# Block-sparse attention and FFN in one kernel: the lead-in's steps in another order, eleven of them ahead of the first unit

## The chip, the cores and the metric

The kernel runs on one core of a Trainium2 chip. The metric is the device time of the whole program in microseconds. Five engines work at the same time, each through its own queue: TensorE (PE; its weight loads are listed as PEld), VectorE (DVE), ScalarE (ACT), GpSimd (POOL) and SyncE (SP), which here issues nearly all DMAs.

## What is computed

Attention over 4 batches, 8 heads, 768 positions and 64 dimensions, with a mask of blocks of 32: a block of queries sees its own block and its neighbours, the first and the last block, and three blocks given as data in `sampled_blocks`. Queries of the first and the last block see all. Then an FFN of 3072 tokens, 512 to 2048 to 512, with h - tanh(h) between.

```python
mask = np.abs(blk_i - blk_j) <= window
mask = mask | (blk_i == 0) | (blk_j == 0) | (blk_i == n_blocks - 1) | (blk_j == n_blocks - 1)
for qb in range(n_blocks):
    for kb in sampled_blocks[qb]:
        mask[qb * block:(qb + 1) * block, kb * block:(kb + 1) * block] = True
...
attn = np.exp(scores)
attn = attn / (np.sum(attn, axis=-1, keepdims=True) + 1e-09)
...
h = x @ w_in
g = h - np.tanh(h)
return (g @ w_out).astype(np.float32)
```

## The kernel before

The tokens are cut into six chunks of 512 (`CHUNKS`: four blocks of 32 for each of 4 batches). The FFN goes through 96 **units**, a unit being one chunk and one tile of 128 of the 2048 inner columns: `first` makes h in bank 4 or 5 of PSUM with 12 products of 128x512, `bent` the function on ScalarE, VectorE and GpSimd in eleven operations (w, t, hs, th, p1, qq, mk, p2, p3, cp, gh, gl), `second` adds another 12 products to banks 0 to 3, two and a half units later. The first eight units are of chunk 0, units 8 to 23 of chunk 1, and so on.

The attention goes through 112 **steps** (class `Unit`): a step is one block of queries and one half-set c (two of the four batches with all heads; K, Q and V are laid out by half-set), and for the edge blocks a third of all keys. A step reads K from `kr`, a buffer of 256 keys that is gathered out of the resident K (`ks`), and V from `vw`, which is gathered by DMA out of HBM. There are two such buffers (`u.i` 0 and 1). A buffer holds three slots for near blocks, the first and the last block, and three sampled blocks; `fresh` copies only what has changed since the buffer's last step, so a step that stays in its half-set fetches one or two near blocks and three sampled ones, and one that changes the half-set fetches everything (seven DMAs of V, seven copies of K or fewer). The sampled ones need indices: `load_samples` fetches the samples and VectorE turns them into offsets (`kx`, `vx`) in some fifteen small operations.

A step then does: `scores` (32 products on PE into two banks), `most` (two maxima on DVE), `exps` (per half one small scaling and two exponentials on ACT), `turn` (eight transposes on PE), `copy` (two copies on ACT), `accum` (64 products on PE with V), `norm` (four operations on DVE) and `put` (a copy on ACT and a subtraction on POOL that hand the result to the FFN as x). The weights come as 64-bit words and are converted in the kernel: `load` fetches a tile, `convert` has three parts on DVE, `split` one operation on ACT and one on POOL.

Every operation is entered into a plan by `at(time, f, ...)`, with a time in units of the FFN, and the plan is sorted and written out. `InOrder` keeps each engine in the order of the plan (the SP queue among them), so the order by hand is the order on the chip; only the waits between engines are found by the framework. Steps below `LEAD` lie ahead of unit 0, by the formula `t(x) = (n + x - T0) * RATE`; those after it have a first time and a spacing by chunk in `BAND`. With `LEAD` 10 and `T0` 10.25, steps 0 to 7 end ahead of unit 0, and 8 and 9 have their `accum` at 0.52 and 1.15. Then six steps of chunk 1 follow at 0.75, 1.89 and so on, 1.14 apart, up to unit 8. Conversions of the first weights stand at four places ahead of unit 0 and at twelve in units 0 to 7 (`CONVA`), with a bank of PSUM for what lies between their parts (`CONVAB`).

The order of the lead-in before: steps 0 to 3 are blocks 1 to 4 of half-set 0, steps 4 to 7 the same blocks of half-set 1, 8 and 9 block 5 of each; the buffers alternate. The SP queue issues K of half-set 0 in four DMAs, Q of step 0, the samples, Q of steps 1 to 3, V of step 0, K of half-set 1 in four DMAs, V of step 1, and then what the plan asks for: Q (four buffers), V of step n+2 after `accum` of step n, and weights. The gathers of K stand on VectorE for steps 0 and 1 and on GpSimd for all others (the sampled blocks always on GpSimd).

Of the kernel before, what the change touches and what calls it, by code (L numbers as in the profile page):

```python
# [23 lines left out]
B, H, S, D = 4, 8, 768, 64  # L24
# [6 lines left out]
CT = 4  # L31

NU = NTOK // P // CT * NFT

LEAD, T0, RATE = 10, 10.25, 0.62
QUICK, TURN, PROD = (0.66, 0.95), 1.0, 1.33
NQ = 4
KEPT = 3
# [8 lines left out]
SEGS = [(0, 0, HALF), (1, 0, HALF), (1, HALF, NFT), (0, HALF, NFT)] + [(n, 0, NFT) for n in range(2, len(CHUNKS))]  # L47
UNITS = [(n, ft) for n, a, b in SEGS for ft in range(a, b)]
ENDS = [sum(b - a for _, a, b in SEGS[: i + 1]) for i in range(len(SEGS))]
BAND = [None, (0.75, 1.14), (22.72, 1.14), (31.87, 1.44), (47.71, 1.44), (63.55, 1.44)]  # L50
EDGES = {3: (0,), 4: (1,), 5: (2, 3)}
LATE = 71.0
CONVA = [0.1, 0.75, 1.4, 2.05, 2.65, 3.31, 3.77, 4.45, 4.91, 6.05, 7.19, 7.62]
CONVAB = [3, 3, 3, 3, 6, 7, 6, 7, 6, 6, 6, 6]
CONVB = 8.35, 0.94

THR2 = 0.16
# [59 lines left out]
class Unit:  # L117
# [3 lines left out]
    def __init__(self, n, c, time, b=None, f=None, k=None, quick=False):  # L121
        self.n, self.c, self.b, self.f, self.k = n, c, b, f, k
        early = n < LEAD
        if early:
            t = lambda x: (n + x - T0) * RATE
            self.t = dict(s=t(0.3), m=t(0.65), e1=t(1.1), e0=t(1.2), turn=t(2.0), c0=t(2.15), c1=t(2.2), pv=t(2.6), norm=t(3.05))
            if n == LEAD - 2:
                self.t.update(pv=0.52, norm=0.6)
            elif n == LEAD - 1:
                self.t.update(turn=0.38, c0=0.43, c1=0.44, pv=1.15, norm=1.25)  # L130
        else:
            t = lambda x: time + x
            turn, prod = QUICK if quick else (TURN, PROD)
            self.t = dict(s=t(0), m=t(0.08), e1=t(0.2), e0=t(0.3), turn=t(turn), c0=t(turn + 0.06), c1=t(turn + 0.05), pv=t(prod), norm=t(prod + 0.1))
        if n < LEAD - 2:
            self.banks = dict(s=((6, 7), (0, 1))[n % 2], t=(2, 3), o=4 + n % 2)
        elif n == LEAD - 1:
            self.banks = dict(s=(0, 1), t=(0, 1), o=2)
        else:
            self.banks = dict(s=(6, 7), t=(2, 3) if early else (6, 7), o=7)  # L140

    def at(self, half, j):

        return (half, self.b) if self.b else (self.f, (NB - 1) * half)


class Attention:
    def __init__(self, tc, k, q, v, samp, rows, ffn, ident, banks, att, sm, f2, rv, at):
# [14 lines left out]

        def add(c, time, **kw):
            u = Unit(len(units), c, time, **kw)
            u.i, u.before = c, last.get(c)
            if u.n < LEAD - 2:
                u.i, u.before = u.n % 2, units[u.n - 2] if u.n > 1 else None
            elif u.n < LEAD:
                u.before = units[u.n - 2]  # L170
            if u.b:
                last[c] = u
            units.append(u)

        for c in range(2):
            for b in CHUNKS[0]:
                add(c, 0, b=b)
        for m, blocks in list(enumerate(CHUNKS))[1:]:
            steps = [(c, dict(b=b, quick=m < 3)) for b in blocks if 0 < b < NB - 1 for c in range(2)]
            edges = [(g // 2, dict(f=g % 2, k=k)) for g in EDGES.get(m, ()) for k in range(3)]  # L180
            steps += edges
            for i, (c, kw) in enumerate(steps):
                add(c, BAND[m][0] + BAND[m][1] * (i - 2 * (m == 1)), **kw)
        lead = lambda x: (x - T0) * RATE
        at(lead(-8.97), self.load_q, units[0])
        for bt in range(B):
            at(lead(-9), self.load_k, 0, bt)
        at(lead(-8.95), self.load_samples, samp, rows)
        for c, t in ((1, lead(-2.5)),):
            for bt in range(B):  # L190
                at(t, self.load_k, c, bt)
        for u in units:
            t, n = u.t, u.n
            if u.b:
                if n:
                    at(max(t["s"] - 2.0, units[n - NQ].t["s"] + 0.01) if n >= NQ else lead(-8.95 + 0.01 * n), self.load_q, u)
                at(max(t["s"] - 1.2, u.before.t["s"] + 0.01 if u.before else lead(-3)), self.gather_k, u)
                at(max(t["s"] - 2.0, u.before.t["pv"] + 0.01 if u.before else lead(-3)), self.gather_v, u)
            else:
                if u.k == 0:  # L200
                    at(units[n - 1].t["s"] + 0.02, self.load_q, u)
                at(units[n - 2].t["pv"] + 0.02, self.load_ve, u)
            at(t["s"], self.scores, u)
            at(t["m"], self.most, u)
            at(t["e1"], self.exps, u, 1)
            at(t["e0"], self.exps, u, 0)
            at(t["turn"], self.turn, u)
            at(t["c1"], self.copy, u, 1)
            at(t["c0"], self.copy, u, 0)
            at(t["pv"], self.accum, u)  # L210
            at(t["norm"], self.norm, u)
            if u.b:
                for x in "hl":
                    at(t["norm"] + (0.1 if x == "h" else 0.15), self.put, u, x)
            elif u.k == 2:
                at(t["e0"] + 0.12, self.weigh, u)
                end = 2 * u.c + u.f in EDGES[len(CHUNKS) - 1]
                quiet = iter([t["norm"] + 0.1 + 0.08 * j for j in range(6)] if end else self.quiet(units[u.n + 1 :], t["norm"]))
                for k in range(3):
                    for s in range(1 + k):  # L220
                        at(next(quiet), self.join, u, k, s)
                for i in range(2):
                    for x in "hl":
                        at(t["norm"] + 0.65 + 0.2 * i if end else LATE + 0.5 * (2 * u.c + u.f) + 0.25 * i, self.put, u, x, i)
# [5 lines left out]
            yield max((u + 0.56 + 0.04 * i for i in range(6)), key=lambda x: min([1] + [abs(x - y) for y in near]))  # L230

    def kr(self, u):
        key = u.i, u.n < 8 + CT * 2
        if key not in self.krs:
            self.krs[key] = self.att.tile([P, H, 256], F32, tag=f"kr{u.i}", name=f"kr{u.i}_{u.n}")
            self.held.pop(("k", u.i), None)
        return self.krs[key]

    def vw(self, u):
        key = u.i, u.n < 8 + CT * 2  # L240
        if key not in self.vws:
            self.vws[key] = [self.att.tile([P, B, VW], F32, tag=f"vw{u.i}{x}", name=f"vw{u.i}{x}_{u.n}") for x in range(2)]
            self.held.pop(("v", u.i), None)
# [8 lines left out]
        return self.loans[i // 2][:, i % 2]  # L252

    def load_k(self, c, bt):
        self.nc.sync.dma_start(out=self.ks[:, c, 2 * bt : 2 * bt + 2], in_=self.k[c][:, 2 * bt : 2 * bt + 2])

    def load_q(self, u):
        for b in (u.b,) if u.b else (0, NB - 1):
# [57 lines left out]
    def gather_k(self, u):  # L316
        nc, i = self.nc, u.i
        k, to = self.ks[:, u.c], self.kr(u)
        e = nc.vector if u.n < 2 else nc.gpsimd
        for s, b, n in self.fresh(("k", i), u, self.near(u) + [(3, 0), (4, NB - 1)]):  # L320
            o = slice(32 * s, 32 * (s + n)) if s < 4 else slice(131, 256, 4)
            e.tensor_copy(out=to[:, :, o], in_=k[:, :, 32 * b : 32 * (b + n)])
# [152 lines left out]
class FFN:  # L475
# [154 lines left out]
    def plan(self, at):  # L630
# [1 line left out]
        banks = [x.bitcast(I32) for x in self.banks]  # L632
        halves = [sorted(((m, ft) for ft in range(a, a + HALF) for m in "io"), key=lambda w: w[1] + NEED[w[0]]) for a in (0, HALF)]
        halves[1].insert(13, halves[1].pop(12))
        slots = [(t(3.3 + 1.6 * k), 0.3 * RATE, None) for k in range(4)] + [(x, 0.09, banks[b]) for x, b in zip(CONVA, CONVAB)]
        slots += [(CONVB[0] + CONVB[1] * k, 0.12, banks[6 + k % 2]) for k in range(2 * HALF)]
        free = []
        for k, ((m, ft), (t0, dt, tmp)) in enumerate(zip(halves[0] + halves[1], slots)):
# [75 lines left out]
```

## Time and profile before

| | us |
|---|---|
| median of three runs | 794.02 (793.66 to 796.94) |
| the profiled execution | 797.82 |
| its span, first to last instruction | 796.1 |
| PE busy in the span | 742.5 (93%) |
| DVE, ACT, POOL busy | 544.1, 478.0, 335.0 |

A span is read in stretches: a table of stages gives the busy time of each engine between two times from the span's start, the chain of waits follows what released what, and the timeline gives instructions in order with the idle time ahead of each and who ended it. Nearly all instructions are issued by one helper, so all have line 78 and are told apart by their tiles: `ps` is a bank of PSUM, `kr<-ks` a gather of K, `vw<-v` one of V, `ps<-kr,q` scores, `m<-ps` most, `ps<-ident,p` turn, `pt<-ps` copy, `ps<-vw,pt` accum, `rs`, `x`, `xt` norm, `ps<-x,wri` the first product of a unit with resident weights, `cvti` and `cvto` the last part of a conversion.

### The profile page before, as it was taken

The page shows a single profiled execution, that of the slowest core. Times are in us where ns is not written, and L with a number is a line of the kernel's source. Part 1 is how long each engine was busy: PE and PEld are TensorE (multiplying, and loading weights), DVE is VectorE, ACT ScalarE, POOL GpSimd, SP SyncE. Part 2 cuts the span into 40 slices and gives each one's busy share as a digit, 9 for nine tenths or more (in the row PEclk, how much of TensorE's full clock was granted, in tenths as well). Part 3 has the DMA queues.
Part 4 walks back from the last instruction along what each step waited for, and adds up shares of the span by engine and source line. Part 5 has one row for each costly group of instructions (what it writes and reads, how often), then busy time and mean ns, then how long its engine had stood idle before and what let it go on. Part 6 is the DMA issues. An engine that isn't in the chain of part 4 may idle for free.

```text
span 796.1 us, 20648 instructions
## 1 busy us (share of the span) xinstructions
PE 742.5 (93%) x8128; PEld 564.5 (71%) x8128; DVE 544.1 (68%) x970; ACT 478.0 (60%) x1021; POOL 335.0 (42%) x406
## 2 busy tenths in 40 slices
PE   0668888999999999999999999999999999999996
PEld 0445656777877777777777777777777777888885
DVE  2565886777986666776666778666676666866654
ACT  0566776667767677566565566565664656554543
POOL 2684666567796555343312334422242211222211
PEclk9878999999999999999999999999999999999998
DMA  7987675399694765475737156666147355236542
GB/s 255 334 226 232 222 226 170 142 331 328 242 276 159 215 216 195 135 230 163 267 115 227 51 173 212 204 224 208 46 129 264 134 200 187 106 106 239 185 159 79
DMA packets 54835, 155.48 MB, mean 195 GB/s; under 512 B 9171, under 2 KB 15828, under 8 KB 54740
## 3 DMA queue, kind: packets, MB, share of 16 engines
q1 hardware_dynamic: 54356, 153.65, 58.7%
q8 instruction: 64, 1.05, 0.5%
q10 hardware_dynamic: 384, 0.52, 0.2%
q14 instruction: 31, 0.25, 0.1%
HBM read 133.17 MB, written 20.97 MB: 194 GB/s over the span
## 4 chain that ended last, share of the span: by engine, by line
PE 75%; DVE 9%; ACT 5%; DMA 4%; POOL 3%; issue 2%; SPq 1%; POOLq 0%; DVEq 0%
PE ps L78 75%; DVE ps L78 4%; DMA vw<-v 2%; ACT pt L78 1%; SPq L78 1%; ACT p L78 1%; DMA ks<-k 1%; DMA room<-rows 1%; DVE m L78 1%; POOL gl L78 1%; DVE cvto L78 1%; POOL kr L78 1%; DVE cvti L78 1%; POOL t L78 1%; DVE t L78 1%
## 5 line engine op out<-in xcount | busy, mean ns | idle before, releaser
L78 PE MATMUL ps<-x,wi 128*128 128x512 f32 x888 | 228.3, 398 | 0.0
L78 POOL TENSOR_TENSOR gl<-t,gh 128x512 fp32r<-128x512 f32 x96 | 124.2, 1294 | 240.4 <-ACT gh L78 123.9
L78 PEld LDWEIGHTS ps<-x,wi 128*128 128x128 f32 x888 | 162.5, 188 | 42.4 <-issue 7.4
L78 PE MATMUL ps<-wo,gh 128*128 128x512 f32 x592 | 190.9, 404 | 0.0
L78 PEld LDWEIGHTS ps<-wo,gh 128*128 128x128 f32 x592 | 107.0, 188 | 30.9 <-issue 7.4
L78 PE MATMUL ps<-wo,gl 128*128 128x512 f32 x296 | 117.0, 397 | 2.8 <-POOL gl L78 2.8
L78 ACT ACTIVATE u<-ps 128x512 f32<-128x512 f32 x96 | 57.2, 596 | 90.1 <-PE ps L78 89.3
L78 POOL COPY kr<-ks 128x256 f32 (+2 forms) x188 | 96.8, 611 | 19.8 <-DVE kr L78 14.5
L78 DVE TENSOR_REDUCE m<-ps 128x2 f32<-128x512 f32 x112 | 72.1, 685 | 40.8 <-PE ps L78 38.4
L78 PE MATMUL ps<-kr,q 64*32 64x256 f32 x1408 | 59.9, 410 | 23.8 <-POOL kr L78 17.9
L78 POOL TENSOR_TENSOR x<-xt,x 128x256 fp32r<-128x256 f32 (+1 forms) x48 | 34.5, 720 | 111.7 <-ACT x L78 108.8
L78 DVE TENSOR_TENSOR ps<-ps,u 128x512 f32<-128x512 f32 x96 | 66.5, 693 | 16.5 <-ACT t L78 16.5
L78 DVE COPY_PREDICATED t<-mk,ps 128x512 f32<-128x512 int32 x96 | 71.4, 743 | 7.4 <-POOL t L78 0.6
L78 ACT ACTIVATE p<-ps,nb 128x256 f32<-128x256 f32 x176 | 73.9, 471 | 3.0
L78 DVE TENSOR_TENSOR t<-t,ps 128x512 f32<-128x512 f32 x64 | 43.7, 683 | 46.6 <-ACT t L78 46.5
L78 DVE SCALAR_TENSOR_TENSOR ps<-qq,ps 128x512 f32<-128x512 f32 x96 | 66.4, 691 | 8.4 <-ACT qq L78 2.7
L78 ACT ACTIVATE qq<-u,bias 128x512 f32<-128x512 f32 x96 | 69.6, 725 | 0.0
L78 ACT ACTIVATE mk<-u,bias 128x512 f32<-128x512 f32 x96 | 69.4, 723 | 0.0
L78 PEld LDWEIGHTS ps<-wo,gl 128*128 128x128 f32 x296 | 55.6, 188 | 18.4 <-POOL gl L78 5.3
L78 DVE SCALAR_TENSOR_TENSOR ps<-u,ps 128x512 f32<-128x512 f32 x96 | 66.3, 691 | 1.9
L78 PEld LDWEIGHTS ps<-vw,pt 128*32 128x32 f32 x2816 | 44.2, 113 | 32.3 <-issue 12.0
L78 ACT ACTIVATE pt<-ps 128x512 f32<-128x512 f32 x72 | 41.5, 598 | 42.5 <-PE ps L78 42.3
(98 smaller groups left out, 1002.0 us busy)
## 6 DMA issues: line engine op xcount, KB each, us to landing
wi<-w2i SPq DMA_DIRECT2D x65, 512.0 KB, 5.3
wo<-w2o SPq DMA_DIRECT2D x65, 512.0 KB, 4.8
vw<-v SPq DMA_DIRECT2D x186, 130.0 KB, 3.2
q<-q SPq DMA_DIRECT2D x52, 128.0 KB, 4.9
ve<-v SPq DMA_DIRECT2D x24, 260.0 KB, 3.7
ks<-k SPq DMA_DIRECT2D x8, 768.0 KB, 7.5
rawo<-w SPq DMA_DIRECT2D x12, 512.0 KB, 4.6
rawi<-w SPq DMA_DIRECT2D x10, 512.0 KB, 4.5
```

Source lines behind the costliest of these rows:

```text
L78: r = f(*args, **kw)
```

## The change

The lead-in has eleven steps, in the order of a list: four of half-set 0, then half-set 1 and half-set 0 in turn. From step 4 on a buffer belongs to a half-set (`u.i = 1 - c`). All eleven end ahead of unit 0, in the banks that the first eight had. Five steps of chunk 1 remain for the band, 1.4 units apart. The samples are issued first, then K of half-set 0 (in two DMAs of 1.5 MB instead of four of 768 KB), Q, V of step 0 and of step 1, and then K of half-set 1, also in two. The copies of K for step 4, the first of half-set 1, go to VectorE. The conversions ahead of unit 0 start at 5.9 steps and stand 1.7 apart (before 3.3 and 1.6); from the fifth on those in the band stand in pairs around the end of a step, all on bank 6.

```diff
-LEAD, T0, RATE = 10, 10.25, 0.62
+LEAD, T0, RATE = 11, 13.22, 0.62
...
-BAND = [None, (0.75, 1.14), (22.72, 1.14), (31.87, 1.44), (47.71, 1.44), (63.55, 1.44)]
+BAND = [None, (0.75, 1.4), (22.72, 1.14), (31.87, 1.44), (47.71, 1.44), (63.55, 1.44)]
...
-CONVA = [0.1, 0.75, 1.4, 2.05, 2.65, 3.31, 3.77, 4.45, 4.91, 6.05, 7.19, 7.62]
-CONVAB = [3, 3, 3, 3, 6, 7, 6, 7, 6, 6, 6, 6]
+CONVA = [0.1, 0.75, 1.4, 2.05, 2.9, 3.25, 4.3, 4.65, 5.7, 6.05, 7.1, 7.45]
+CONVAB = [3, 3, 3, 3, 6, 6, 6, 6, 6, 6, 6, 6]
+FIRSTS = [(0, 1), (0, 2), (0, 3), (0, 4), (1, 1), (0, 5), (1, 2), (0, 6), (1, 3), (0, 7), (1, 4)]
...
-            if n == LEAD - 2:
-                self.t.update(pv=0.52, norm=0.6)
-            elif n == LEAD - 1:
-                self.t.update(turn=0.38, c0=0.43, c1=0.44, pv=1.15, norm=1.25)
...
+        self.banks = dict(s=((6, 7), (0, 1))[n % 2], t=(2, 3), o=4 + n % 2) if early else dict(s=(6, 7), t=(6, 7), o=7)
...
+            u.i = u.n % 2 if u.n < 4 else 1 - c
+            u.before = last.get(u.i)
             if u.b:
-                last[c] = u
+                last[u.i] = u
...
-        for c in range(2):
-            for b in CHUNKS[0]:
-                add(c, 0, b=b)
+        for c, b in FIRSTS:
+            add(c, 0, b=b)
...
-        for bt in range(B):
+        for bt in range(2):
             at(lead(-9), self.load_k, 0, bt)
-        at(lead(-8.95), self.load_samples, samp, rows)
+        at(lead(-9.1), self.load_samples, samp, rows)
         for c, t in ((1, lead(-2.5)),):
-            for bt in range(B):
+            for bt in range(2):
                 at(t, self.load_k, c, bt)
...
-                at(max(t["s"] - 2.0, u.before.t["pv"] + 0.01 if u.before else lead(-3)), self.gather_v, u)
+                at(max(t["s"] - 2.0, u.before.t["pv"] + 0.01) if u.before else lead(-3 + 0.1 * n), self.gather_v, u)
...
-        self.nc.sync.dma_start(out=self.ks[:, c, 2 * bt : 2 * bt + 2], in_=self.k[c][:, 2 * bt : 2 * bt + 2])
+        self.nc.sync.dma_start(out=self.ks[:, c, 4 * bt : 4 * bt + 4], in_=self.k[c][:, 4 * bt : 4 * bt + 4])
...
-        e = nc.vector if u.n < 2 else nc.gpsimd
+        e = nc.vector if u.n < 2 or u.n == 4 else nc.gpsimd
...
-        slots = [(t(3.3 + 1.6 * k), 0.3 * RATE, None) for k in range(4)] + [(x, 0.09, banks[b]) for x, b in zip(CONVA, CONVAB)]
+        slots = [(t(5.9 + 1.7 * k), 0.3 * RATE, None) for k in range(4)] + [(x, 0.09, banks[b]) for x, b in zip(CONVA, CONVAB)]
```

## Rows read from the trace of the kernel before

**Rows 1.** Table of stages: length, busy PE, PEld, DVE, ACT, POOL (count), clock, DMA, GB/s.
```profile
33.00:71.00 38.00, 28.28 (x683) 20.14 (x683) 24.54 (x52) 21.76 (x60) 23.82 (x36) 0.76 0.83 237
...
71.40:148.90 77.50, 67.67 (x932) 47.84 (x931) 56.59 (x108) 53.29 (x118) 47.41 (x57) 1.00 0.61 193
...
157.00:216.00 59.00, 58.23 (x247) 45.63 (x246) 48.94 (x76) 41.18 (x75) 41.63 (x34) 1.00 0.85 303
```

**Rows 2.** Timeline, DVE and POOL, lead-in: start, length, instruction, [idle before, who ended it].
```profile
10.97 0.18 DVE L78 CAST room<-room 1x66 f32<-1x66 int32 x1 [10.05 <-DMA room<-samp]
...
14.43 2.46 DVE L78 COPY kr<-ks 128x768 f32<-128x768 f32 x7
...
28.92 3.21 POOL L78 COPY kr<-ks 128x768 f32<-128x768 f32 x6 [4.64 <-DMA ks<-k]
...
33.89 0.95 DVE L78 TENSOR_SCALAR tmpi<-rawi 128x512 int32<-128x512 int32 x1 [6.52 <-DMA rawi<-w]
...
35.65 1.28 DVE L78 TENSOR_REDUCE m<-ps 128x2 f32<-128x512 f32 x2
```

**Rows 3.** Timeline, PE, lead-in: start, length, instruction, [idle before, who ended it].
```profile
17.92 3.67 PE L78 MATMUL ps<-kr,q 64*32 64x256 f32 x64 [17.92 <-POOL kr L78]
...
26.92 1.09 PE L78 MATMUL ps<-kr,q 64*32 64x256 f32 x32
...
32.68 2.01 PE L78 MATMUL ps<-vw,pt 128*32 128x65 f32 x56 [0.61 <-DMA vw<-v]
...
40.18 1.46 PE L78 MATMUL ps<-vw,pt 128*32 128x65 f32 x64 [2.17 <-ACT pt L78]
...
49.98 1.00 PE L78 MATMUL ps<-vw,pt 128*32 128x65 f32 x56 [1.23 <-DMA vw<-v]
...
59.21 1.74 PE L78 MATMUL ps<-vw,pt 128*32 128x65 f32 x56 [2.24 <-DMA vw<-v]
...
64.67 1.11 PE L78 MATMUL ps<-vw,pt 128*32 128x65 f32 x64
...
69.46 1.18 PE L78 MATMUL ps<-vw,pt 128*32 128x65 f32 x64 [1.62 <-ACT pt L78]
...
71.42 1.62 PE L78 MATMUL ps<-x,wri 128*128 128x512 f32 x6
```

**Rows 4.** Issue to landing: K's first four (0 to 16), V's first seven (8 to 19).
```profile
DMA to landing us min/median/max: 4.4/7.2/8.6
...
DMA to landing us min/median/max: 2.4/2.8/4.3
```

**Rows 5.** Timeline, SP queue, lead-in: start, length, DMAs issued.
```profile
0.75 2.10 SPq L78 DMA_DIRECT2D ks<-k  x4
...
17.19 2.23 SPq L78 DMA_DIRECT2D ks<-k  x4
...
31.98 2.56 SPq L78 DMA_DIRECT2D vw<-v  x4
...
41.46 6.54 SPq L78 DMA_DIRECT2D vw<-v  x7
```

**Rows 6.** Waits of the SP queue, 0 to 75: total us, times, longest.
```profile
SPq L78 <- DMA ks<-k: 10.2, 8, 2.3
```

**Rows 7.** Groups by shape, 71 to 149: count, busy us, mean ns, idle before.
```profile
L78 ACT ACTIVATE p<-ps,nb 128x256 f32<-128x256 f32 x28 | 11.8, 471 | 0.5
...
L78 ACT ACTIVATE pt<-ps 128x512 f32<-128x512 f32 x16 | 8.8, 596 | 2.1 <-PE ps L78 2.0
...
L78 DVE TENSOR_SCALAR ps<-rawi 128x512 int32<-128x512 int32 x4 | 2.8, 692 | 4.9 <-ACT pt L78 4.9
```

**Rows 8.** Timeline, PE, in the band: two scores, and unit 8's start.
```profile
101.19 1.09 PE L78 MATMUL ps<-kr,q 64*32 64x256 f32 x30 [0.17 <-DVE x L78]
...
113.15 1.09 PE L78 MATMUL ps<-kr,q 64*32 64x256 f32 x30 [0.71 <-DVE x L78]
...
148.89 2.91 PE L78 MATMUL ps<-x,wri 128*128 128x512 f32 x12
```

More of the change, by code (lines that the diff above doesn't have):

```diff
@@ L134, in __init__ @@
             self.t = dict(s=t(0), m=t(0.08), e1=t(0.2), e0=t(0.3), turn=t(turn), c0=t(turn + 0.06), c1=t(turn + 0.05), pv=t(prod), norm=t(prod + 0.1))
[L135 to L140, printed above, removed]
+        self.banks = dict(s=((6, 7), (0, 1))[n % 2], t=(2, 3), o=4 + n % 2) if early else dict(s=(6, 7), t=(6, 7), o=7)
     def at(self, half, j):
@@ L165, in add @@
             u = Unit(len(units), c, time, **kw)
[L166 to L170, printed above, removed]
+            u.i = u.n % 2 if u.n < 4 else 1 - c
+            u.before = last.get(u.i)
             if u.b:
-                last[c] = u
+                last[u.i] = u
             units.append(u)
-        for c in range(2):
-            for b in CHUNKS[0]:
-                add(c, 0, b=b)
+        for c, b in FIRSTS:
+            add(c, 0, b=b)
         for m, blocks in list(enumerate(CHUNKS))[1:]:
-            steps = [(c, dict(b=b, quick=m < 3)) for b in blocks if 0 < b < NB - 1 for c in range(2)]
+            steps = [(c, dict(b=b, quick=m < 3)) for b in blocks if 0 < b < NB - 1 for c in range(2) if (c, b) not in FIRSTS]
             edges = [(g // 2, dict(f=g % 2, k=k)) for g in EDGES.get(m, ()) for k in range(3)]
@@ L182, in __init__ @@
             for i, (c, kw) in enumerate(steps):
-                add(c, BAND[m][0] + BAND[m][1] * (i - 2 * (m == 1)), **kw)
+                add(c, BAND[m][0] + BAND[m][1] * i, **kw)
         lead = lambda x: (x - T0) * RATE
         at(lead(-8.97), self.load_q, units[0])
-        for bt in range(B):
+        for bt in range(2):
             at(lead(-9), self.load_k, 0, bt)
-        at(lead(-8.95), self.load_samples, samp, rows)
+        at(lead(-9.1), self.load_samples, samp, rows)
         for c, t in ((1, lead(-2.5)),):
-            for bt in range(B):
+            for bt in range(2):
                 at(t, self.load_k, c, bt)
@@ L232, in kr @@
     def kr(self, u):
-        key = u.i, u.n < 8 + CT * 2
+        key = u.i, u.n < 16
         if key not in self.krs:
@@ L239, in vw @@
     def vw(self, u):
-        key = u.i, u.n < 8 + CT * 2
+        key = u.i, u.n < 16
         if key not in self.vws:
```

## The prediction

> **What bounds the kernel now.** I read the table of stages first [rows 1]. From 157 us on TensorE is busy 98.7% of the time at the full clock, so whatever is gained or lost earlier is carried to the end unchanged, and the question is when unit 8 starts (148.9). Ahead of that lie two stretches with different limits. In the lead-in (to 71.4) the long waits end with loads: K's gather at 28.92, accum at 32.68, 49.98 and 59.21 [rows 2, 3]. From 33 us on TensorE works 28.3 of 38.0 us at a granted clock of 0.76 [rows 1]. In the band (units 0 to 7, 71.4 to 148.9, 77.5 us) no engine is full: PE 67.7, DVE 56.6, ACT 53.3, POOL 47.4 [rows 1]; the steps there go one after the other through all engines. A step is scores, most, exps, turn, copy, accum, norm; "accum(5)" is that stage of step 5.
>
> The execution profiled has a span of 796.1 us and took 797.82, which is 3.8 above the median of the runs (794.02). Everything is summed as a difference at the start of unit 8 and put onto the median.
>
> **Samples first.** VectorE sat idle until the samples landed at 10.95, worked on the indices, and began its copies of K at 14.43 [rows 2]: 3.6 us after K was there (four K loads issued from 0.75, 0.5 apart, the last one landing after 8.6, [rows 4, 5]). Ahead of K, the samples cost K two small issues, 0.6 us at the 0.56 of a K load or less each [rows 5]; K is there at 11.4 with the indices done. The copies start 3.0 us sooner, and scores(0) moves from 17.92 [rows 3] to 14.9. Everything up to the end of scores(3) moves with it, from 28.0 [rows 3] to 25.1.
>
> **Both V sets ahead of the other K.** The queue stops for landings: 10.2 us in eight waits for K loads [rows 6]. So all but a few loads of V are issued only after K is in: ten after 11.4, at 0.64 us each with their register loads (2.56 for four, [rows 5]), then the other K, at 18.3 instead of 17.19 [rows 5]. V of step 1 lands by 18.3 + 4.3 = 22.6 at the latest [rows 4], ahead of accum(1), which waited for it till 32.68 [rows 3]. The other K took from 17.19 [rows 5] to 28.9 [rows 2], 11.7; the first K from 0.75 [rows 5] to 10.8, 10.05. From 18.3 that gives 28.4 to 30.0; I take **29.0**, as the queue behind it holds fewer V loads than before.
>
> **The wait that is added.** Step 4's fixed copies go to VectorE now, and in the plan they stand right behind scores(2), ahead of most(2), norm(0), most(3) and norm(1). They wait for the other K. Behind most(2) hang exps(2), and behind these on ScalarE copy(1), so accum(1) too. That a waiting VectorE lets nothing pass is in the rows: a conversion waited for its raw weights till 33.89, and most(3), whose scores had ended at 28.0, ran at 35.65 behind it [rows 2, 3]. So: 29.0 + copies 1.1 (three of the seven that took 2.46, [rows 2]) + half a most 0.7 [rows 2] + exps 1.1 + copy 1.2 [rows 7] = 33.1 for the start of accum(1). I give it 2.0 as before, since TensorE will have been idle as long and the clock fell to 1.2 GHz then (2.01 against 1.11 later, [rows 3]). It ends at 35.1; before 34.7. (scores(4) itself needs the sampled copies on GpSimd too, 1.6 more as six took 3.21, so 31.7 [rows 2]: earlier than TensorE comes to it.) **V ahead of K buys nothing at this place.** The Trainium skill, PSUM — Partial Sum Buffer, section Engine vs sequencer instructions, has it that the queues of ScalarE, VectorE and GpSimd are strict FIFO; by that the wait counts whole, as the rows have it. If VectorE could pass it, scores(4) would come from K alone and the sum below would be 4 us smaller.
>
> **Steps 2 to 4.** turn(2) 2.0, scores(4) 1.5, accum(2) 1.1 to 1.5: 39.8. Before, accum(2) ended at 41.6 (start 40.18, after 2.17 of waiting for copies that stood behind the early weight conversion, [rows 3]); the conversions start later now. Step 4 changes the half-set of its buffer, so its whole V set of seven loads follows accum(2); before, 8.4 us lay between that end and the last landing at 49.98 [rows 3]. (V of step 3, four loads behind accum(1), lands by 35.1 + 2.6 + 4.3 = 42.0, and accum(3) is not due before 43.) So accum(4) starts at 48.2 and ends at 49.3 (before 51.0).
>
> **Step 5.** Its buffer keeps its half-set: four loads in place of seven. They are issued behind those of step 4 (6.54 for seven and 2.56 for four, [rows 5]: till 48.9) and land 2.4 to 4.3 later [rows 4], 3.7 taken: accum(5) ends at 53.7. Before, it waited for V till 59.21 and ended at 60.95 [rows 3]. This is the gain of the lead-in, **7.2 us**.
>
> **Steps 6 to 10.** Before, two steps remained after step 5; now five. Unstalled accums stood 4.8 apart with a weight conversion between (64.67 to 69.46, [rows 3]). ScalarE bounds the period from below: four p at 0.47, two pt at 0.6 [rows 7] and three small ones, 3.6. Four conversions, 1.7 steps apart, touch about three of the five, and a conversion is spread over more than a step: between 3.6 and 4.8 I take 4.15. accum(10) ends at 53.7 + 20.7 = **74.4**, and unit 0 starts there; bounds 71.7 and 77.7. Before it started at 71.42 [rows 3]. So the lead-in costs 3.0 us more, with accum(8), turn(9), accum(9) and the whole of step 10 done in it.
>
> **The band.** Five steps instead of six and the remains of two. On TensorE that is 6.5 us less (three accums, two turns and one scores of 1.1), on VectorE about 5 (three norms and one most). But the steps stand 1.4 units apart instead of 1.14, and each takes two conversions with it, both on bank 6, which the scores use: the next scores wait for the second. I walked through the queues by hand, in the order of the plan, with 0.69 for each of a conversion's three parts, 0.6 for an ACT of 128x512 [rows 7], a little more where it reads SBUF. From unit 0's start: scores(11) at 4.1, scores(12) at 15.2, scores(13) at 33.4, scores(14) at 47.1, scores(15) at 61.0, unit 8 at 74.0. The first period is scores 1.2, most 1.3, p1 and two parts of a conversion 2.1, then on ScalarE the split behind it, mk and the second exps 2.4, turn 1.0, copy 1.1, accum 1.1, norm as far as x 0.8: 11.0. The second is long: on VectorE the rest of norm, p1, p2 and two parts of a conversion (3.2) stand ahead of most(12), which ends at 4.5, and the third part ends at 5.2; on ScalarE the split behind that part, four p, w, hs, t, gh and two pt follow (6.2: 11.4); then a conversion with p2 between (2.8), norm 0.8, the rest of norm and the second conversion with p3 between (3.2): 18.2. The usual one: scores 1.2; on ScalarE, after split, w, hs and t beside scores and most, two p, gh, two p, qq, mk and two pt, till 7.6; conversion 2.1, cp 0.7, norm 0.8, rest and second conversion 2.5: 13.7. The last runs till copy the same way (8.2), then accum 1.1, a quarter of first 0.7 and second 2.8: 13. The same walk gives 12.0 for a period of before; scores stood 11.96 apart (101.19 to 113.15, [rows 8]). So **74.0** against 77.5. Bounds: 70.1, if PE keeps its share of 0.873 (67.7 less 6.5, divided by it, [rows 1]), and 77.5, if a unit takes what it took. I take the walk, nearest to rows 7 and 8.
>
> **Sum.** 74.4 + 74.0 = 148.4 against 148.9: -0.5, so **793.5**. Two changes of some microseconds cancel.
>
> **The rivals.** (1) The band returns the work taken out of it: 70.1, unit 8 at 144.5, 4.4 sooner, **789.6**. For it: every engine there has idle time, and fewer serial steps need fewer of the waits. Against: the walk, in which the second conversion on bank 6 fills the gap. 0.24.
> (2) Fewer, larger K loads land sooner. If each load paid the 2.5 us that the first took beyond its stream (4.4 less 1.9), two instead of four would bring the other K 5.0 sooner and all behind it: **788.5**. Against: first and last of K landed at 5.15 and 10.8, 1.9 apart for 768 KB [rows 4]; the fixed part overlaps. 0.07. The Trainium skill, DMA: Bandwidth & Descriptors, section Bandwidth, asks for transfers of 1 MiB and more; its fit would make two of 1.5 MB an estimated 4 us shorter than four of 768 KB, and the spacing in rows 4 doesn't bear that out.
> (3) Slower: V keeps stalling. A step's V can only be fetched after the accum two steps before it, and one fetch with its wait took 8.4 [rows 3]. If four loads take as long as seven did, the period is (1.1 + 8.4)/2 = 4.75 at least, and 6.0 if each also waits for the other buffer's issue of 2.56; before, accum(1) to accum(7) averaged 6.1 (32.68 to 69.46, [rows 3]). At 5.5 the six steps 5 to 10 cost 8 us more: **801.5**. It decides from 4.9 a step on. For it: it was the limit of the whole lead-in. Against: only one full change of half-set is left of two, and 2.4 to 4.3 us to landing where no K is in the way [rows 4]. 0.25.
> That the change doesn't do what it says holds for one part, V ahead of K, and is in the forecast.
>
> **How the numbers follow.** Forecast, no change: 0.44. Measurement here tells apart about 0.5%, 4 us: 790 and 798. Faster: rivals 1 and 2, 0.31. Slower: rival 3, 0.25. Bounds of the terms: 71.7 + 70.1 gives 786.9; 77.7 + 77.5 gives 800.3. The range takes these and about half of rival 3: 786.5 to 801.0; the forecast alone has 790 to 798.
>
> **What would show it.** Right: scores(0) near 15; VectorE's copies for step 4 waiting for K till about 29 with the mosts behind; accum(5) ending near 54; unit 0 at 72 to 78; scores(13) to scores(15) near 13.8 apart; unit 8 near 148. Wrong: most(2) ahead of the other K's landing; V waits of over 1 us in steps 6 to 10; a band of 70 or less; any difference growing after 157 us.

## The result, and the profile after

The changed kernel takes **806.35 us** (median of 4, 805.51 to 806.79) against 795.03 for the kernel before beside it (793.66 to 796.94): a ratio of 1.0138, 95% interval 1.0118 to 1.0158. It is 11.3 us slower; forecast was no change, at 793.5, with a range that ended at 801.0. The profiled execution took 806.02 with a span of 803.9, so 7.8 more than the span of before, and near its own median, where that of before (797.82) lay 2.8 above 795.03. The profiles thus hold 8 of the 11 us. A time that is read from a profile, such as the start of unit 0, is called a mark below.

The stages first, as in [rows 1]: lead-in, band, and the part behind it, each with its length, busy PE, PEld, DVE, ACT, POOL (count), granted clock, DMA share and GB/s.

```profile
33.00:81.59 48.59, 34.74 (x937) 24.97 (x937) 30.97 (x74) 33.04 (x88) 28.07 (x43) 0.82 0.63 193
81.59:154.99 73.40, 62.51 (x688) 45.42 (x688) 52.47 (x94) 46.98 (x100) 42.42 (x47) 0.92 0.56 181
163.00:222.00 59.00, 58.38 (x247) 46.33 (x246) 47.42 (x74) 39.64 (x73) 39.94 (x32) 0.99 0.82 295
```

Unit 0 starts at 81.59 instead of 71.42 [rows 3], the band takes 73.4 us instead of 77.5 (at a granted clock of 0.92 instead of 1.00), and what follows is as full of TensorE as before. The loss is in the lead-in. Its timeline of TensorE (start, length, instruction, count, idle time before it and what ended that), to be laid beside [rows 3]:

```profile
14.06 1.96 PE L79 MATMUL ps<-kr,q 64*32 64x256 f32 x32 [14.06 <-POOL kr L79]
...
19.34 1.09 PE L79 MATMUL ps<-kr,q 64*32 64x256 f32 x32
...
23.30 1.09 PE L79 MATMUL ps<-kr,q 64*32 64x256 f32 x32
35.66 1.98 PE L79 MATMUL ps<-vw,pt 128*32 128x65 f32 x64 [11.26 <-ACT pt L79]
37.56 1.97 PE L79 MATMUL ps<-ident,p 128*128 128x128 f32 x8
39.46 1.96 PE L79 MATMUL ps<-kr,q 64*32 64x256 f32 x32
41.35 1.25 PE L79 MATMUL ps<-vw,pt 128*32 128x65 f32 x64
...
50.64 1.00 PE L79 MATMUL ps<-vw,pt 128*32 128x65 f32 x56 [2.20 <-DMA vw<-v]
...
56.04 1.00 PE L79 MATMUL ps<-vw,pt 128*32 128x65 f32 x56 [0.55 <-issue]
```

The lines at 19.34 and 23.30 are scores(2) and scores(3). scores(0) starts 3.9 us sooner than before, and then TensorE stands still for 11.26 us ahead of accum(1). Why is in the timelines of VectorE and of the SP queue, and in the landing times of K's loads (three of the four are recorded; when the last one landed is read from the start of VectorE's copy at 31.08):

```profile
18.29 1.29 DVE L79 TENSOR_REDUCE m<-ps 128x2 f32<-128x512 f32 x2 [0.84 <-PE ps L79]
31.08 1.94 DVE L79 COPY kr<-ks 128x768 f32<-128x768 f32 x3 [11.51 <-DMA ks<-k]
32.87 1.25 DVE L79 TENSOR_REDUCE m<-ps 128x2 f32<-128x512 f32 x2
```

```profile
4.35 15.40 SPq L79 DMA_DIRECT2D vw<-v  x14
19.80 1.06 SPq L79 DMA_DIRECT2D ks<-k  x2
```

```profile
DMA to landing us min/median/max: 6.3/7.0/9.6
```

The 14 loads of the two V sets hold the SP queue from 4.35 to 19.75: two of them stop for landings of the first K (5.6 us in all), and eleven are issued only from 11.49 on, behind the second of these; the other K follows at 19.80, and VectorE's first copy of it starts at 31.08. most(2), whose scores had ended at 20.4, waits behind that copy.

From accum(5) on the steps come 4.73 us apart ((80.6 - 56.97)/5, from the end of accum(5) to the end of accum(10)); this distance is called the period. Seven lines from there, of the same timeline of TensorE, the start of unit 0 last, then the stage from 75.65 to 80.63:

```profile
60.89 1.00 PE L79 MATMUL ps<-vw,pt 128*32 128x65 f32 x56 [0.61 <-DMA vw<-v]
...
65.08 1.23 PE L79 MATMUL ps<-vw,pt 128*32 128x65 f32 x56 [0.66 <-DMA vw<-v]
...
70.67 1.00 PE L79 MATMUL ps<-vw,pt 128*32 128x65 f32 x56 [0.99 <-DMA vw<-v]
...
74.72 1.00 PE L79 MATMUL ps<-vw,pt 128*32 128x65 f32 x56 [0.53 <-DMA vw<-v]
75.65 1.84 PE L79 MATMUL ps<-ident,p 128*128 128x128 f32 x8
78.67 1.96 PE L79 MATMUL ps<-vw,pt 128*32 128x65 f32 x64 [1.18 <-ACT pt L79]
81.59 1.65 PE L79 MATMUL ps<-x,wri 128*128 128x512 f32 x3 [0.95 <-DVE x L79]
```

```profile
75.65:80.63 4.98, 3.81 (x78) 3.16 (x72) 1.21 (x4) 1.39 (x3) 3.12 (x6) 0.52 0.72 209
```

Every accum from 4 to 9 stops after its first eight matmuls, all but accum(5) until V lands by the profile, those of the steps 6 to 9 for 2.8 us in all. In step 10 the granted clock was 0.52, close to its lower level of 1.2 GHz, and turn(10) and accum(10) took 1.84 and 1.96 us where they take 1.09 and 1.11 at the full clock (in a_nov), 1.6 us more. Before it fell, TensorE had worked 2.3 of 4.1 us (71.60 to 75.65), with the last wait for V in that stretch; in a_nov and a_wl, without V's waits, the clock stayed full there. Waits and clock together are 4.4 us of the 23.6 in these five steps. And ahead of unit 0 stands a wait of 0.95 that was not in the forecast: step 10's output lies in PSUM bank 4, which is also the bank of unit 0's h, so unit 0 waits until VectorE has read it.

### The profile page after: what moved, and what is told of

It reads as the page before. It is cut to its first block, busy times and chain, and to the rows that moved or that the text cites. A ratio compares the mean times of both kernels' runs of the same rounds, so it can differ in the third digit from the quotient of the medians.

```text
span 803.9 us, 20627 instructions
## 1 busy us (share of the span) xinstructions
PE 743.1 (92%) x8128; PEld 566.9 (71%) x8128; DVE 547.3 (68%) x973; ACT 478.7 (60%) x1021; POOL 332.0 (41%) x397
## 4 chain that ended last, share of the span: by engine, by line
PE 73%; DVE 10%; ACT 6%; DMA 5%; SPq 2%; issue 2%; POOL 2%; POOLq 0%; DVEq 0%; ACTq 0%
PE ps L79 73%; DVE ps L79 5%; DMA ks<-k 3%; SPq L79 2%; DMA vw<-v 1%; DVE cvto L79 1%; ACT pt L79 1%; ACT t L79 1%; ACT p L79 1%; ACT u L79 1%; DMA spare<-w 1%; DVE cvti L79 1%; POOL gl L79 1%; ACT hs L79 1%; DVE m L79 1%
## 5 line engine op out<-in xcount | busy, mean ns | idle before, releaser
L79 POOL COPY kr<-ks 128x256 f32 (+2 forms) x179 | 93.7, 618 | 20.9 <-DMA ks<-k 20.9
L79 PE MATMUL ps<-kr,q 64*32 64x256 f32 x1408 | 56.7, 411 | 22.1 <-POOL kr L79 14.5
L79 PE MATMUL ps<-vw,pt 128*32 128x65 f32 x2816 | 53.0, 227 | 22.8 <-ACT pt L79 16.0
```

Of the source, the lines that this page charges most:

```text
L79: r = f(*args, **kw)
```

## The experiments

All times stand beside runs of the kernel before on the same chip; the marks are from one profile each. The other K's second load landed at 31.0 in the profile of the changed kernel and 1.5 to 2.5 us later in five kernels with the same head of the queue, so a difference of 2 us between two profiles' marks proves nothing. The profiles of a_k10, x1 and x5 are of the fastest executions of these kernels (793.88, 795.22 and 791.89), so their marks look better than their medians. The kernel before took 795.03 to 796.42 in the median of these lots, so medians of two lots compare to about 1 us; the ratios don't have this error. Where time and mark disagree I say so.

| kernel | median us | ratio to before, interval | unit 0 starts |
|---|---|---|---|
| changed kernel | 806.35 | 1.0138 (1.0118 to 1.0158) | 81.59 |
| a_regs | 804.32 | 1.0097 (1.0069 to 1.0126) | 82.47 |
| a_bank | 805.91 | 1.0132 (1.0098 to 1.0166) | 83.50 |
| a_kpool | 800.69 | 1.0072 (1.0049 to 1.0094) | 77.68 |
| a_k1 | 800.01 | 1.0049 (1.0026 to 1.0072) | 78.02 |
| a_nov | 800.31, one run | | 79.78 |
| a_wl | 802.37 | 1.0097 (1.0072 to 1.0123) | 79.17 |
| x1 | 797.52 | 1.0028 (1.0007 to 1.0050) | 72.00 |
| x2 | 797.44 | 1.0031 (1.0004 to 1.0058) | 75.56 |
| x3 | 795.47 | 0.9987 (0.9968 to 1.0005) | 72.42 |
| a_k10 | 797.73 | 1.0018 (0.9995 to 1.0040) | 73.15 |
| x5 | 794.76 | 0.9990 (0.9972 to 1.0008) | 70.71 |
| x5_again | 793.83 | 0.9978 (0.9958 to 0.9998) | 72.23 |
| x6 | 794.54 | 0.9982 (0.9970 to 0.9995) | 72.32 |
| b_samp | 795.01 | 0.9993 (0.9974 to 1.0013) | 66.64 |
| b_k10 | 794.33 | 0.9972 (0.9954 to 0.9991) | 68.78 |

### The wait of VectorE for the other K

**a_kpool**: the fixed copies of step 4 leave VectorE.

```diff
-        e = nc.vector if u.n < 2 or u.n == 4 else nc.gpsimd
+        e = nc.vector if u.n < 2 else nc.gpsimd
```

> The changed kernel, but step 4's fixed copies of the other K go to GpSimd instead of VectorE. Theory A (VectorE's wait for the other K holds up most(2) and with it accum(1) and all that follows): most(2) runs near 21 to 27 instead of 32.9, accum(1) starts before 30 instead of at 35.7, accum(2) ends near 36 instead of 42.5, accum(4) ends at 45 to 46 instead of 51.6, unit 0 moves by 4 to 6 us and the time falls by as much. Theory B (the steps behind are set by V's fetches and give it back): accum(1) and accum(2) come sooner, but unit 0 moves by less than 2 us. Theory C (GpSimd is slower, three copies of K and three sampled ones after the landing): scores(4) comes 2 us later than now and accum(4) with it: 0 to 2 us slower.

TensorE in that stretch, and GpSimd's first line of the other K:

```profile
24.72 1.23 PE L79 MATMUL ps<-vw,pt 128*32 128x65 f32 x64
25.88 1.09 PE L79 MATMUL ps<-ident,p 128*128 128x128 f32 x8
36.21 1.96 PE L79 MATMUL ps<-kr,q 64*32 64x256 f32 x32 [9.24 <-DMA vw<-v]
38.10 1.96 PE L79 MATMUL ps<-vw,pt 128*32 128x65 f32 x64
```

```profile
32.95 3.21 POOL L79 COPY kr<-ks 128x768 f32<-128x768 f32 x6 [12.24 <-DMA ks<-k]
```

accum(1) starts at 24.72 instead of 35.66, so VectorE's wait was what held it. But accum(2) starts only at 38.10: it stands behind scores(4) on TensorE, and scores(4) needs the other K whatever engine copies it (32.95 + 3.21 = 36.16; the timeline names V for that gap, but scores(4) does not read V). The same wait has moved one engine on, so accum(2) ends at 40.1 and accum(4) at 48.6, not at 36 and 46 as theory A had it; of 10.9 us at accum(1) 3.9 are left at unit 0 and 5.7 in the time (5.2 by the ratios), about theory A's amount.

### The place of the other K in the queue

**a_k1** and **a_k10** put the two loads between the V sets, and ahead of both.

```diff
-        for c, t in ((1, lead(-2.5)),):
+        for c, t in ((1, lead(-2.95)),):
```

> The changed kernel, but the two loads of the other K are issued between the V sets of step 0 and of step 1 instead of behind both. Theory A (the other K's landing starts everything from step 1 on): K is issued 3 us sooner, lands at 28 instead of 30.96, accum(1) starts at 32.7 instead of 35.7, and unit 0 and the time come 2 to 3 us sooner. Theory B (the V set of step 1, now behind 3 MB of K, takes K's place): V of step 1 lands at 30 to 33, accum(1) and unit 0 move by less than 1 us.

```diff
-        for c, t in ((1, lead(-2.5)),):
+        for c, t in ((1, lead(-3.05)),):
```

> The changed kernel with the other K ahead of both V sets. Its two loads then stand in the queue before the V loads that stop for the landing of the first K, so they are issued near 4.5 instead of 19.8 and land one behind the other at 19 to 21 instead of 31 to 33; V of step 0 lands at 23 to 24 instead of 18, V of step 1 by 27. Theory A (the other K's landing, through VectorE's wait, is what the lead-in lost): accum(0) comes 2 to 3 us later, but accum(1) at 26 to 28 instead of 35.7, unit 0 at 73 to 75, and the time 796 to 799. Theory B (the V sets, now late, hold up as much): accum(1) not ahead of 32, unit 0 at 78 or later, the time 801 or more.

SP queue, VectorE and TensorE of a_k10:

```profile
4.41 0.97 SPq L79 DMA_DIRECT2D ks<-k  x2
7.82 18.88 SPq L79 DMA_DIRECT2D vw<-v  x14
```

```profile
21.20 1.96 DVE L79 COPY kr<-ks 128x768 f32<-128x768 f32 x3 [1.39 <-PE ps L79]
23.00 1.25 DVE L79 TENSOR_REDUCE m<-ps 128x2 f32<-128x512 f32 x2
```

```profile
23.51 0.45 PE L79 MATMUL ps<-vw,pt 128*32 128x65 f32 x8 [2.46 <-DMA vw<-v]
...
30.18 1.11 PE L79 MATMUL ps<-vw,pt 128*32 128x65 f32 x64
```

The two loads wait for nothing, so ahead of V they are issued at 4.4 and not at 19.8. VectorE finds K there when it comes to the copies (it waits for TensorE, not for a load). accum(0) now waits for V and starts 2.4 us later; accum(1) follows at 30.18 instead of 35.66, a little later than theory A had it, behind turn(2) and scores(4) at the lower clock (1.97 and 1.64 us). Unit 0 starts at 73.15 and the time is 797.73: **one line takes 8.6 of the 11.3 us back** (9.5 by the ratios). Theory A. Not all of that is won ahead of unit 0: the band, whose plan is the same, takes 69.6 us here instead of 73.4, at a granted clock of 0.98 instead of 0.92, with TensorE busy for 59.0 us instead of 62.5:

```profile
73.15:142.76 69.61, 58.96 (x689) 43.29 (x689) 52.53 (x94) 46.80 (x100) 42.39 (x47) 0.98 0.60 195
```

With a_k1 K is issued at 15.5; accum(1) starts at 32.45, and its wait is ended by V of step 1, which now stands behind K. So the wait is theory B's, the gain (unit 0 3.6 us sooner, the time 6.3, or 7.1 by the ratios) more than theory A's 2 to 3.

### V's waits in steps 4 to 10

**a_nov** leaves three loads of each of the steps 6 to 10 out, and with them the SP queue's reads of index registers for these steps:

```diff
+        if 6 <= u.n <= 10:
+            return
         for r, x in enumerate(self.values(mybir.EngineType.SP, self.vx, u, S)):
```

> The changed kernel without the three loads of sampled V of each of the steps 6 to 10 (they multiply by the rows left from the step before, so this part of the computation is left out). Theory A (V's fetch sets the steps): accum no longer stops inside or ahead for V, and the steps 6 to 10 come 3.7 to 4.0 us apart instead of 4.73, so unit 0 starts at 77 to 78 instead of 81.6. Theory B (TensorE's own order and the copies set them: turn 1.1, scores 1.1, accum 1.1, and where no scores lie between, 1.2 of copy): V's waits are only in the slack of that, the period stays above 4.5 and unit 0 at 80.5 or later.

```profile
65.60 1.47 PE L79 MATMUL ps<-vw,pt 128*32 128x65 f32 x64
...
71.08 1.11 PE L79 MATMUL ps<-vw,pt 128*32 128x65 f32 x64 [1.86 <-ACT pt L79]
...
74.40 1.11 PE L79 MATMUL ps<-vw,pt 128*32 128x65 f32 x64 [1.17 <-ACT pt L79]
```

accum runs through, and the steps come 3.88 us apart ((78.8 - 59.4)/5): the fetch of V cost 0.85 a step, 4.3 in five, the waits and the clock (2.8 and 1.6) together. Theory A in the period; unit 0 comes only at 79.78, since in this run accum(5) ended 2.4 us later, K having landed later. What is left of the period is mostly TensorE's order: turn 1.09, scores 1.09, accum 1.11 and, where no scores lies between turn and accum, 1.17 of waiting for the copy. Three of the five accums follow 3.3 us after the one before; accum(8) follows after 5.5, with 1.86 of waiting for the copy.

V is late although it is only four loads a step. One reason lies in the queue that issues them, which is nearly full. From 48.7 to 76.2, when it issues what the steps 5 to 10 need, the SP queue waited for 2.9 of 27.5 us in the changed kernel (the only line of its waits there):

```profile
SPq L79 <- PE ps L79: 2.9, 5, 1.3
```

The rest it spent issuing V, Q and weights and reading registers; in a_bank it waited for 0.5 us of the same stretch. Two candidates for what fills it needlessly. **a_regs**: the index registers. `values` kept one group of four blocks, and from step 4 on the order alternates between two groups, so every step reads them anew. All register loads of the changed kernel, then of a_regs, SP's line each:

```profile
L277 SPq TENSOR_LOAD <-vx x12: 738/750/1205, 12.1 to 555.2; - x12
```

```profile
L277 SPq TENSOR_LOAD <-vx x6: 743/753/1204, 12.0 to 556.5; - x6
```

```diff
-        if self.vals.get(eng, (None,))[0] != b0:
+        if (eng, b0) not in self.vals:
...
-            self.vals[eng] = b0, vals
+            self.vals[eng, b0] = vals
...
-        return self.vals[eng][1][o : o + 3]
+        return self.vals[eng, b0][o : o + 3]
```

> The changed kernel, but the index registers of a group of four blocks stay loaded on each queue once they are read, so that steps 4 to 10, which alternate between two groups, read them twice per queue instead of once per step. Theory A (the reloads stretch the steps): seven reloads of 0.75 us on SP go, the steps 6 to 10 come 4.0 to 4.2 us apart instead of 4.73, unit 0 starts at 77 to 79 instead of 81.6, and the time falls by 3 to 4 us. Theory B (the round of accum, V fetch, accum sets the steps, and most reloads lie under a wait for the accum): only the two reloads that stand in the chain of waits count, 1.5 us at unit 0, and the time falls by 0 to 2 us. Theory C (ScalarE and the order on TensorE set the steps): under 0.5 us.

Six loads of 0.75 us are gone, and the period is 4.44 ((81.5 - 59.3)/5): 0.3 a step, 1.5 in five. That is theory B's amount, but about 1.0 of it is the clock (of the last step only the end of accum(10) ran at the lower one here), and the accums of the steps 6 to 10 waited 4.0 us for V, more than the 2.8 in the changed kernel. The time fell by 2.0 (3.3 by the ratios), with intervals that overlap. So what the reload costs by itself is not shown.

**a_wl**: the weight loads in the same queue.

```diff
-            at(max(t0 - 1.8, free[k - 3] if k > 2 else -99), self.load, m, ft, k)
+            at(slots[0][0] - 1.8 + 0.01 * k if k < 4 else max(t0 - 1.8, free[k - 3]), self.load, m, ft, k)
```

> The changed kernel, but the four weight loads of the lead-in (512 KB each) are issued together right behind V of step 2, while the queue waits for accum(1), instead of one per step between the V sets of steps 4 to 10. Theory A (V lands late because a weight load of 2 to 2.5 us stands ahead of it in the queue): the landings of V in the steps 5 to 10 come 2 to 3 us after issue instead of 4 to 5, the gaps of accum for V shrink from about 0.65 to under 0.2 each, unit 0 starts 2.5 to 4 us sooner and the time falls by as much. Theory B (the weights then collide with V of steps 2 to 4): accum(4) ends 1 to 3 us later than 51.6, and unit 0 moves by less than 1.5 us.

DMA issues of the changed kernel from 54 to 72 us, then of a_wl from 52 to 71: how many, KB each, median us from issue to landing.

```profile
vw<-v SPq DMA_DIRECT2D x17, 130.0 KB, 3.3
spare<-w SPq DMA_DIRECT2D x1, 512.0 KB, 4.7
```

```profile
vw<-v SPq DMA_DIRECT2D x18, 130.0 KB, 2.8
```

Without weights between them the V loads land half a microsecond sooner in the median, the accums of the steps 6 to 10 run through, and the period is 4.04 ((78.2 - 58.0)/5), 0.69 less a step. This stretch holds as much work at the lower clock as that of the changed kernel (turn(6) and scores(8) took 1.97 and 1.78 instead of 1.09 each), so the two compare. Unit 0 comes 2.4 us sooner and the time falls by 4.0 (3.3 by the ratios, whose intervals overlap by a little): theory A. The loads of one queue land in the order of their issue here, so V landed after the 512 KB that stood ahead of it. But each weight load also takes 0.4 to 0.6 us of the queue to issue, and a_wl takes both away at once: which of the two counts is not shown.

### The bank

**a_bank**:

```diff
-        self.banks = dict(s=((6, 7), (0, 1))[n % 2], t=(2, 3), o=4 + n % 2) if early else dict(s=(6, 7), t=(6, 7), o=7)
+        self.banks = dict(s=((6, 7), (0, 1))[n % 2], t=(2, 3), o=4 + n % 2 if n < LEAD - 1 else 0) if early else dict(s=(6, 7), t=(6, 7), o=7)
```

> The changed kernel, but the last step ahead of unit 0 (step 10) puts its output into PSUM bank 0 instead of bank 4, which is also the bank of unit 0's h. If the wait of 0.95 us between accum(10) and unit 0 comes from that bank, unit 0 follows accum(10) at once, or waits only for the operand it multiplies; its start moves from 81.6 to 80.7 and the time falls by about 1 us. If unit 0 needs the normed output of step 10 all the same, nothing moves.

```profile
81.61 1.96 PE L79 MATMUL ps<-vw,pt 128*32 128x65 f32 x64 [1.18 <-ACT pt L79]
83.50 2.58 PE L79 MATMUL ps<-x,wri 128*128 128x512 f32 x7
```

The wait of 0.95 is gone: unit 0 follows accum(10) at once. Its mark is later all the same (VectorE's first copy of the other K came at 33.47 in this run, 2.4 later), and of the microsecond the times show 0.4, which is inside the interval.

### Together, and in the kernel before

**x1** is a_kpool, a_k1 and a_bank at once; **x2** adds the edit of a_wl to x1, **x3** that of a_regs.

> The changed kernel with three of the edits at once: step 4's fixed copies on GpSimd, the other K's loads between the V sets of steps 0 and 1, step 10's output in bank 0. If the landing of the other K is the one clock of the steps behind it and the edits add up: scores(4) at 32 to 33 (36.2 with the first edit alone), unit 0 at 72.5 to 74, unit 8 at 146 to 147, the time 793 to 796, which is the kernel before within 0.3%. If the two gains are the same one (each only takes VectorE's wait away), unit 0 stays at 77 and the time at 799 to 801.

> The three edits at once, and the four weight loads of the lead-in issued together behind V of step 2. If weights ahead of V lengthen the steps: unit 0 2.5 to 4 us sooner than with the three edits, at 70 to 71, the time 790 to 792. If the weights now collide with V of steps 2 to 4, the same or 2 us later than with the three edits.

> The three edits at once (fixed copies on GpSimd, the other K between the V sets, step 10's output in bank 0) and the index registers kept. With the three edits the sampled V loads of the steps 7 to 10 stand behind a reload of 0.75 us while the queue is behind the work, so here the reload counts: unit 0 at 69 to 70.5 instead of 72.0, the time 1.5 to 2.5 us less than with the three edits. If the alternating waits for the accum hide it as in the changed kernel: within 1 us of the three edits.

x1 adds up at unit 0, which starts at 72.0 (72.5 to 74 expected), though scores(4) comes at 34.3 (32 to 33 expected); the time, 797.52, is 1.5 above the range. In x2 it goes as the second case had it: V of step 3 stands behind the weights now and lands from 41.5 to 42.6, accum(3) waits for it and ends at 44.5 instead of 40.8 in x1, unit 0 starts 3.6 us later, and the time is the same. With x3 the time is 0.4% better than with x1, with intervals that just miss each other, the mark is not: of the kept registers in this company I can only say that they don't hurt.

**x5** is a_k10, a_bank and a_regs; **x6** moves the second weight load up beside the first.

> The changed kernel with the other K ahead of both V sets, step 10's output in bank 0 and the index registers kept; the fixed copies stay on VectorE, which has nothing to wait for now. If the landing of the other K was the whole loss of the lead-in ahead of accum(4): unit 0 at 70 to 72, the time 792 to 795, level with the kernel before or a little under it. If the V sets hold it up instead: unit 0 at 76 or later, the time 799 or more.

> The same kernel as x5, once more beside the two others: how far its time against the kernel before is from 1. From the ten executions of x5: 0.999, between 0.997 and 1.001.

> The changed kernel with the other K ahead of both V sets, step 10's output in bank 0, the index registers kept, and the second weight load issued beside the first one instead of between the V sets of steps 4 and 5. If that load is what V of step 5 stands behind there: accum(5) ends at 48 to 49 instead of 50.5, unit 0 at 68.5 to 70 instead of 70.7, the time 1 to 2 us less than without. If V of step 3, now behind two weight loads, gives it back: unit 0 at 70.5 to 72, the time the same.

In its two lots x5 is level with the kernel before or 0.2% under it, so with the other K's place, the bank and the registers mended the whole loss is made up. x6 equals it: accum(5) ends 1.5 us sooner (49.9 against 51.4 in x5_again), accum(7) 1.0, and from accum(8) on nothing is left (64.9 against 64.6; unit 0 at 72.32 against 72.23). What takes it back is the clock: between accum(7) and accum(8) TensorE's turn and scores took 1.96 and 1.83 us in x6, and 1.09 each in x5_again. So x6 does not show what that load's place is worth.

**b_samp** and **b_k10** make the kernel before with the samples ahead of K, and with the other K ahead of V as well.

> The kernel before with one part of the change alone: the samples loaded ahead of K. Theory A (the first steps gain, the rest is set by the landings of V and of the other K, and these two do not move): scores(0) starts near 15 instead of 17.9, unit 0 stays within 1 us of 71.4, the time within 0.2% of before. Theory B (the 3 us go through): unit 0 at 68 to 69, the time 0.3 to 0.4% shorter.

> The kernel before (ten steps, its old order) with the samples ahead of K and the other K ahead of both V sets. Theory A (the position of the other K's loads in the queue counts, whatever the order of the steps): the other K lands at 21 to 22 instead of 28.8, accum(1) starts at 28 to 29 instead of 31.6, step 4's copies no longer stand behind K, unit 0 at 63 to 66 instead of 71.4 (66.6 with the samples alone), the time 789 to 793. Theory B (the kernel before has the weights' conversions and V's full sets as its limit): unit 0 at 66 to 71, the time 794 to 796.

b_samp is inconclusive: unit 0 at 66.64 speaks for theory B, the time (0.9993) for theory A; the execution profiled took 793.89, where that of the kernel before took 797.82, so the two marks are not of like executions. b_k10 goes as theory B had it in mark and time, though 0.28% are gained. What it still waits for is mostly V, on TensorE for 13.1 us from 25 to 70 (total, times, longest). On VectorE the conversion of [rows 2] still waits for its weights, with most(3) behind it:

```profile
PE ps L78 <- DMA vw<-v: 13.1, 6, 4.5
```

```profile
31.08 0.70 DVE L78 TENSOR_SCALAR tmpi<-rawi 128x512 int32<-128x512 int32 x1 [3.32 <-DMA rawi<-w]
...
32.51 1.27 DVE L78 TENSOR_REDUCE m<-ps 128x2 f32<-128x512 f32 x2
```

With the other K at the same place in the queue old and new order end level (b_k10 0.9972, x5_again 0.9978, the latter with bank and registers mended too). Both lie under the kernel before, by less than the half per cent that counts here.

## Why the prediction was wrong

**Samples first: right.** scores(0) at 14.06 (14.9 forecast), and lost again, since accum(1) waits for other things.

**The other K: right in kind, 2 us off.** Issue at 19.8 instead of 18.3 (where ten loads at 0.64 from 11.4 on, as written, give 17.8): eleven loads were left, and between V's fixed and sampled loads the queue also reads its registers, which held up the next load till 13.49. VectorE's copies then took 1.94 where I had 1.1 from the shorter copies of [rows 2]. accum(1) starts 2.6 us later than forecast (35.66 for 33.1) and accum(2) ends 2.8 later (42.6 for 39.8). The prediction saw that V ahead of K bought nothing at this place, and did not ask what it would bring to have K ahead of V: 8.6 us, by a_k10. The forecast priced it as a delay of 1.1 us against the kernel before. The Trainium skill, PSUM — Partial Sum Buffer, section Engine vs sequencer instructions, calls the queue of VectorE strict FIFO; the row at 31.08 agrees, most(2) coming 12.4 us after its scores, and a_kpool shows TensorE's queue doing the same one step later.

**accum(4) and accum(5): 2.3 and 3.3 late**, the 2.8 from above less 0.5, then 1.0 more for V of step 5. The term of 7.2 that step 5 was to gain is there in kind (60.95 became 56.97), 4.0 in size.

**The period of the steps 6 to 10: the step that failed in kind.** 4.15 was taken from ScalarE and the conversions; 4.73 was measured, 2.9 us in five steps. The forecast had put V's waits at nothing here, because four loads with no K in the way land after 2.4 to 4.3 us [rows 4]. That time runs only from the issue. It left out what stands ahead of the issue in the same queue, the loads of Q, the four weight loads of 512 KB and the reads of registers: a_nov and a_wl show that without V's waits the period is 3.9 to 4.0. Rival 3 was right here, in its price of 4.75 and in its condition: from the end of the accum that frees the buffer to the moment when the accum that waits for V goes on it took 8.0 us in step 7 (57.04 to 65.08), 8.8 in step 8 and 8.4 in step 9, so four loads took as long as the 8.4 of seven before. By itself that is under the 4.9 a step at which rival 3 was to decide; the time left the range because it came on top of the rest. ScalarE's 3.6 was no lower bound for a single step either, as three accums of a_nov follow 3.3 apart.

**Unit 0: 81.59 for 74.4.** 3.3 up to accum(5), 2.9 in the period (1.6 of them the clock in step 10, which the forecast had not reckoned with), 0.95 for bank 4. The bank was in the diff (o = 4 + n % 2 now also for the last step) and was overlooked.

**The band: right in the sum, in part by luck.** 73.4 for 74.0, but scores(12) to scores(13) took 16.1 where the walk had 18.2, and scores(15) to unit 8 took 14.7 where it had 13. And the walk was made at the full clock, while the band ran at 0.92: in a_k10 and a_nov, at 0.98, it took 69.6, which is rival 1's time. So the walk was some 4 us too long for a band at nearly the full clock.

**The rest is not quite rigid.** Unit 8 starts 6.1 later than before, and 1.7 more are lost by the start of unit 10. Table of stages, 12 us around unit 8: the changed kernel, a_bank, and the kernel before.

```profile
153.00:165.00 12.00, 9.03 (x31) 6.61 (x31) 10.90 (x18) 8.30 (x16) 8.70 (x8) 0.86 0.58 204
```

```profile
153.00:165.00 12.00, 9.65 (x42) 7.28 (x41) 10.86 (x20) 8.78 (x16) 7.93 (x7) 1.00 0.53 179
```

```profile
147.00:159.00 12.00, 10.12 (x44) 7.94 (x43) 11.09 (x20) 8.78 (x16) 8.61 (x8) 1.00 0.54 197
```

TensorE waited 2.36 us for GpSimd's gl there (1.88 in the kernel before), and the granted clock fell to its lower level behind that gap (0.86 over the stretch); a_bank has the same gap, 2.35, and keeps the full clock. Why it fell in the one and not in the other stays open.

**Rival 2** falls: the first K, in two loads of 1.5 MB, was issued from 1.43 and there at 11.48, 10.05 us, as long as in four [rows 4, 5]. The Trainium skill, DMA: Bandwidth & Descriptors, section Bandwidth, asks for 1 MiB and more; it measured loads issued from GpSimd, and for these, issued from SyncE, the runs show no gain from going from 768 KB to 1.5 MB.

**From marks to the time.** 7.2 us late at unit 0, 0.6 regained in the band and 1.7 behind unit 8 make 8.3 of the 12.9 us by which 793.5 was missed. The other 4.5 come from the step that put differences of one profile onto the median: the span of before (796.1) lay 2.1 above that median, the span of the changed kernel (803.9) 2.4 below its own. No run tells which stage they belong to.

## To carry to other kernels

A load that waits for nothing belongs in a queue ahead of those that stop for landings, however late its data are due: here that line was worth 8.6 us, and the wait that it caused showed on VectorE, then on TensorE, while the queue itself waited for only 5.6 us. Before a fetch is called hidden, list everything that shares its queue and add up what the queue needs to issue it: two loads that are each small enough can be late together. And when a change alternates between two sets, look at each cache that was sized for one (registers, a bank, a buffer).

## What the runs showed of the hardware

Loads of one queue landed in the order of their issue in these rows, so a V load of 130 KB behind weight loads of 512 KB took up to 4.7 us from issue to landing where it took 2.3 with no weights on their way ahead of it (all V loads of the changed kernel from 30 to 82 us):

```profile
DMA to landing us min/median/max: 2.3/3.0/4.7
```

A read of twelve index registers held SP for 0.75 us and GpSimd for 0.81 us in the median. Two K loads of 1.5 MB took as long as four of 768 KB, 10.05 us. At a granted clock of 0.52 the same turn and accum took 1.84 and 1.96 us instead of 1.09 and 1.11.
